# Summing the heads of O during attention for the last eight projection visits, and smaller moves around it, in an adaLN transformer block

## The chip, the cores and the metric

The kernel runs on one core of a Trainium2 chip. The metric is the time of one execution on the device in microseconds; the median of several runs counts. The engines are TensorE (PE in the profile; PEld is its loading of weights), VectorE (DVE), ScalarE (ACT), GpSimd (POOL) and SyncE (SP), whose queue issues almost all DMAs here. Each engine works through its own instructions in the order in which they were issued, and waits on semaphores for the others.

## The reference, cut to what matters

```python
mod = (silu(c) @ w_mod).reshape(1, 6, 1, -1)          # sa, ca, ga, sb, cb, gb
h = layernorm(x) * (1 + ca) + sa                      # x: 2048 x 576
q = (h @ wq), 32 heads of 128; k, v: last 512 keys of 16 cached heads, each used by 2 heads
o = softmax(q k^T * 128 ** -0.5) v                    # per head
x = x + ga * (o @ wo)                                 # wo: 4096 x 576
h = layernorm(x) * (1 + cb) + sb
x = x + gb * ((sigmoid(h @ w_gate) * (h @ w_up)) @ w_down)   # 576 -> 4608 -> 576
```

All in float32.

## The kernel before, in words

A float32 operand of a matmul is split into a high part of a shorter format (F32R) and the rest, and a product is three matmuls: high by low, low by high, high by high (`three`, L280). The split costs an ACT copy (high part) and a subtraction on DVE or POOL (low part).

**Order.** The work is traced in a written order, and a planner then orders the instructions of each engine by when it expects their inputs. An instruction that is pinned (`pin`, L112, and `keep_order`, L108, while `held` is set) stays behind the instruction traced before it on its engine. In attention everything hangs on a step counter n from -8 to beyond N = 512 (loop at L948): `at_n(n, f)` calls f at the beginning of step n, `at_late(n, f)` at its end.

**Attention** (L948 to L978). The 2048 rows are four blocks of 512, in two halves (blocks 0 and 1, then 2 and 3). A unit b is one head on one block (128 in all, `seq` at L415: head by head, in each half), and takes four steps, one for each 128 rows. In step n PE works on q for two units ahead (`qproj`), scores and row maximum for two steps ahead (`scores`; the maximum on DVE, tile neg), the exponential (`expo`, ACT, tile pp), the transposes of this step (`transp`; ACT and DVE split them into ptt) and P times V of the unit before (`pv`, into ot). After a unit's last exponential DVE takes the reciprocal of the sums (rs). It has to be spread over the partitions: `put_rs` and `get_rs` write it to DRAM and read it back as a broadcast tile rb; for the last two units, `spread_rs` (L544) multiplies it into an identity (dg) and `spread_mm` (L549) multiplies that by ones on PE, and ACT copies the result to rb. At the end of `pv` DVE multiplies ot by rb into ov, which holds one head for both blocks, and `put_o` (L556) stores it in oscr.

**Beside attention**, the weights of wo, w_gate, w_up and w_down are combined into the sums that the later products need and split (jobs of `bg_load`, `bg_sums`, `bg_split`, `bg_store`, planned at L817 to L839; they use the four tiles of x, one a room, whose content isn't needed then). `norm_block` (L648) makes the statistics (`ln_stats`, L178), the chain of small DVE operations that turns a variance into 1 / sqrt (`ln_chain`, L192, by bit tricks and three Newton steps), the normalised rows (`ln_apply`) and their transposes for blocks 2 and 3 in the steps before half time. `shift_cols` (L855) makes columns of the second shift.

**Projection of O** (L1263 to L1280). The product by wo goes by a scheme of seven products for a 2 x 2 by 2 x 2 product (rows: two blocks; columns: two halves of 288; inner: even and odd heads). There are 32 visits v: 8 passes over (quarter of the heads q, pair of blocks p) by 4 row tiles t. A visit loads 1 MB of O (`v_load`, L907), makes three sums and one in-place difference of its four planes (`v_sum`, L912), splits seven planes (`v_split`, L925: tile vh, three buffers) and runs seven stages of twelve matmuls, each followed by a DVE add from PSUM to x. `beside(v, s)` (L1220) traces what goes beside stage s: a sum and a split for the next visit and, towards the end, the weights of the next quarter (`w_load`, L893, from wosc, pinned on SP), the statistics of blocks 0 and 1 on DVE and their normalising for the MLP (`early_norm`, `early_scale`, `early_sum`).

**MLP** (L1291 on). For each pair of blocks 36 column blocks of 128, with the same scheme of seven products; weights come 192 KB at a time (`load_w`: sr), are split (`split_w`: sw) and used in `product`. The second pair's rows are normalised meanwhile (`late_load`, `late_tile`, L1187 to L1216) and their parts stored.

Of the kernel before, what the change touches and what calls it, by code (L numbers as in the profile page):

```python
# [44 lines left out]
def adaln_block_kernel(ctx: ExitStack, tc: tile.TileContext, x, k_cache, v_cache, wq, wo, w_gate, w_up, w_down,  # L45
# [127 lines left out]
    def load_x(b):  # L173
        keep_order(nc.sync.dma_start(xs[b], xf[b]))
# [17 lines left out]
    def ln_chain(b, both):  # L192
        sl = slice(0, 2) if both else slice(b % 2, b % 2 + 1)
        mv, y, v, a = [z[:, sl] for z in LN[b][2]]
        yi, vi = y.bitcast(I32), v.bitcast(I32)
        ops = [lambda: nc.vector.tensor_scalar(v, mv[:, :, :, 1], EPS, None, op0=OP.add),
# [6 lines left out]
        ops += [lambda: nc.vector.scalar_tensor_tensor(a, mv[:, :, :, 0], -1.0, y, op0=OP.mult, op1=OP.mult)]  # L203
# [281 lines left out]
    def expo(n):  # L485
# [58 lines left out]
    def spread_rs(b):  # L544
        DG[b] = at.tile([P, TPB, P], F32, tag="qt", name="dg", bufs=2)
        for i in range(TPB):
            nc.vector.tensor_scalar(DG[b][:, i], ident, RS[b][:, i : i + 1], None, op0=OP.mult)

    def spread_mm(b):  # L549
        p = ps_qp()  # L550
        for i in range(TPB):
            nc.tensor.matmul(p[:, i * P : (i + 1) * P], ones, DG[b][:, i], start=True, stop=True)
# [3 lines left out]
    def put_o(b):  # L556
        half, hd, blk = blk_of(b)
        to = oscr[half][hd // 8][:, :, hd // 2 % 4, 2 * (hd % 2) : 2 * (hd % 2) + 2]
        keep_order((nc.scalar if b == NBLK - 1 else nc.sync).dma_start(to, OT.pop((half, hd))))
# [83 lines left out]
    for b in range(2, NB):  # L643
        at_n(N // 2 - 43 + b, load_x, b)
    for b in range(NB):
        at_n(N - 48 + 4 * b, load_x, b)

    def norm_block(b, n_stats, n_apply, n_t, step, sc_, sh_, mul, add):  # L648
# [4 lines left out]
        for k in range(12):  # L653
            at_n(n_stats + TPB + k, ln_some, b, False, k, k + 1)
# [3 lines left out]
    norm_block(2, n1 - 35, n1 - 19, n1 - 14, 2, scale, shift, nc.gpsimd, nc.gpsimd)  # L658
# [10 lines left out]
    EX = {}  # L669
# [10 lines left out]
    def early_scale(t, b):  # L680
        h = xs[b][:, t, :]
        (nc.vector if b else nc.gpsimd).tensor_mul(h, h, rows2["scale"])

    def early_sum(t, k):
        if k == 0 and t % 2 == 0:
            for c in (T1, T2, T4):
                EX[c, t // 2] = hp.tile([P, 2, D2], F32, tag="ts", name="ex", bufs=6)
# [131 lines left out]
    while jobs or wide:  # L819
# [10 lines left out]
        for r in rooms:  # L830
            free[r] = n + {"ab": 10, "tail": 13}.get(kind, 12)
        at_n(n, bg_load, k, rooms)
        for part in range(2):
            at_n(n + 4 + part, bg_sums, k, part)
            if kind != "ab":
                at_n(n + 6 + part, bg_split, k, part)
        for part in range(4 if kind == "tail" else 1):
            at_n(n + (7 if kind == "ab" else 8) + part, bg_store, k, part)
        due = max(due, n - 2) + {"ab": 4.6, "tail": 7.6}.get(kind, 5.9)  # L839

# [13 lines left out]

# [587 lines left out]
```

## Time and profile before

| | |
|---|---|
| median of 3 runs | 3082.87 us (3081.51 to 3083.08) |
| the profiled execution | 3081.02 us, its span 3079.0 us |
| granted TensorE clock, mean | 0.997 |
| instructions | 49150 |
| POOL, ACT busy in the span | 1641.9 us, 1680.2 us |
| DMA packets moved | 558.72 MB, mean 181 GB/s |

A row of the timeline gives start and duration in us, engine, operation, output<-input by the program's tile names, shape, how many were merged, and in brackets how long the engine was idle before it and what ended that. Rows of groups (one line of code, engine, operation, tiles) give the busy us, the mean ns of one, the idle us before them. Every instruction has the line L36, that of the helper that records it, so that tiles tell them apart. SPq is SP issuing a DMA; the duration is the issuing, not the transfer. The granted clock is the share of full speed that TensorE got.

### The profile page before, as it was taken

The numbers are of one execution on the slowest core, as the hardware profiler recorded it, in microseconds if no ns is written. First come the engines' busy times: TensorE is split into PE (matmuls) and PEld (weight loads), VectorE is DVE, ScalarE is ACT, GpSimd is POOL, SyncE is SP. The second block draws the span as 40 slices with busy tenths as digits, with TensorE's granted clock in tenths as the row PEclk, the third lists the DMA queues.
The fourth block names the chain that finished last, engine by engine and source line by source line (L and its number), as shares of the span: only waits on it lengthen the run. The fifth ranks groups of instructions, "written<-read, shape, count | busy, mean of one in ns | idle before, by whom it ended". The sixth has DMA issues, their size and how long they took to land.

```text
span 3079.0 us, 49150 instructions
## 1 busy us (share of the span) xinstructions
PE 3022.5 (98%) x16651; PEld 2600.9 (84%) x16651; DVE 2190.9 (71%) x3872; ACT 1680.2 (55%) x3358; POOL 1641.9 (53%) x1534
## 2 busy tenths in 40 slices
PE   8999999999999999999999999999999999999998
PEld 6888788878888888887999888888888888888887
DVE  6666666677666666667888987666666876666667
ACT  5666666656667676554334454444544545444542
POOL 2334368644577773212555327666655666555654
PEclk9999999999999999999999999999999999999999
DMA  4687778766777777654546535555555564554453
GB/s 124 182 199 213 193 235 249 218 183 185 194 250 249 249 238 185 174 172 169 204 160 263 214 125 173 170 158 163 166 148 142 159 187 135 148 146 142 135 159 100
DMA packets 468795, 558.72 MB, mean 181 GB/s; under 512 B 51136, under 2 KB 421056, under 8 KB 459584
## 3 DMA queue, kind: packets, MB, share of 16 engines
q1 hardware_dynamic: 467408, 555.06, 60.1%
q8 instruction: 132, 2.16, 0.3%
q14 instruction: 119, 0.97, 0.1%
q10 hardware_dynamic: 1136, 0.53, 0.1%
HBM read 388.04 MB, written 167.41 MB: 180 GB/s over the span
## 4 chain that ended last, share of the span: by engine, by line
PE 87%; DVE 5%; POOL 3%; issue 2%; ACT 1%; DMA 1%; SPq 0%; POOLq 0%; ACTq 0%; DVEq 0%
PE a L36 19%; PE st L36 17%; PE qp L36 13%; PE w L36 12%; PE ot L36 11%; PE c L36 10%; PE b L36 5%; DVE x L36 1%; POOL x L36 1%; DVE vh L36 1%; POOL hl L36 0%; PE wo L36 0%; POOL vs L36 0%; DVE neg L36 0%; ACT pp L36 0%
## 5 line engine op out<-in xcount | busy, mean ns | idle before, releaser
L36 DVE TENSOR_TENSOR x<-w,x 128x288 f32<-128x288 f32 x980 | 435.6, 454 | 299.7 <-PE w L36 295.8
L36 PE MATMUL a<-hc,sw 128*128 128x512 f32 x2016 | 584.9, 395 | 9.2 <-POOL sw L36 5.2
L36 DVE TENSOR_REDUCE neg<-st 128x1 f32<-128x512 f32 x512 | 352.7, 689 | 281.1 <-PE st L36 281.1
L36 ACT ACTIVATE ptt<-st 128x512 fp32r<-128x512 f32 x512 | 306.2, 598 | 394.3 <-PE st L36 393.9
L36 PE MATMUL ot<-ptt,vs 128*128 128x512 f32 x1536 | 487.2, 425 | 2.9 <-DVE ptt L36 2.9
L36 PE MATMUL qp<-hTm,wa 128*128 128x512 f32 x1536 | 446.1, 399 | 4.9 <-DVE qt L36 2.8
L36 PE MATMUL st<-kt,qt 128*128 128x512 f32 x1536 | 443.0, 395 | 1.4 <-ACT pp L36 1.4
L36 DVE TENSOR_TENSOR ptt<-st,ptt 128x512 fp32r<-128x512 f32 x512 | 352.2, 688 | 123.4 <-ACT ptt L36 123.0
L36 ACT ACTIVATE sw<-sr 128x384 fp32r<-128x384 f32 x504 | 261.7, 521 | 261.9 <-issue 91.3
L36 PEld LDWEIGHTS a<-hc,sw 128*128 128x128 f32 x2016 | 355.9, 188 | 51.0 <-POOL sw L36 6.5
L36 ACT ACTIVATE pp<-st,neg 128x512 f32<-128x512 f32 x512 | 350.8, 685 | 55.6 <-DVE neg L36 55.1
L36 POOL TENSOR_TENSOR sw<-sr,sw 128x256 fp32r<-128x256 f32 x252 | 195.0, 775 | 325.1 <-ACT sw L36 228.9
L36 PEld LDWEIGHTS qp<-hTm,wa 128*128 128x128 f32 x1536 | 284.2, 188 | 74.2 <-DVE qt L36 8.3
L36 PEld LDWEIGHTS w<-wh,hl 128*128 128x128 f32 x1776 | 299.3, 189 | 54.8 <-DVE x L36 6.0
L36 PEld LDWEIGHTS st<-kt,qt 128*128 128x128 f32 x1536 | 288.5, 189 | 66.6 <-ACT pp L36 2.4
L36 PE MATMUL w<-wh,hl 128*128 128x288 f32 x1776 | 332.9, 298 | 3.4 <-DVE x L36 3.3
L36 POOL TENSOR_TENSOR x<-x 128x256 f32<-128x256 f32 (+3 forms) x334 | 246.9, 758 | 152.0 <-DMA x<-in_B_w_up_dram 88.4
L36 PEld LDWEIGHTS st<-ident,pp 128*128 128x128 f32 x2048 | 255.8, 140 | 78.0 <-issue 7.2
L36 PE MATMUL st<-ident,pp 128*128 128x128 f32 x2048 | 307.9, 273 | 9.2 <-DVE rs L36 6.4
L36 PE MATMUL c<-hc,sw 128*128 128x512 f32 x1008 | 303.8, 394 | 0.0
L36 PEld LDWEIGHTS ot<-ptt,vs 128*128 128x128 f32 x1536 | 253.5, 191 | 29.7 <-DVE ptt L36 4.2
L36 POOL TENSOR_TENSOR hl<-vs,hl 128x512 fp32r<-128x512 f32 x139 | 186.7, 1343 | 98.9 <-ACT hl L36 98.9
(211 smaller groups left out, 5107.1 us busy)
## 6 DMA issues: line engine op xcount, KB each, us to landing
sr<-wsc SPq DMA_DIRECT2D x504, 192.0 KB
wh<-dsc SPq DMA_DIRECT2D x144, 288.0 KB
dsc<-x SPq DMA_DIRECT2D x34, 1008.0 KB
vr<-oscr SPq DMA_DIRECT2D x32, 1024.0 KB
rb<-rscr SPq DMA_DIRECT2D x126, 256.0 KB
wsc<-x SPq DMA_DIRECT2D x36, 896.0 KB
oscr<-ov SPq DMA_DIRECT2D x63, 512.0 KB
wosc<-x SPq DMA_DIRECT2D x32, 1008.0 KB
```

What stands on the lines that cost most here:

```text
L36: i = got(*args, **kw)
```

## The change

- *Sums of O.* For the second half's heads 16 to 31 (quarters 2 and 3, the last eight visits) the three sums and the difference are made on POOL in attention, when a pair of heads is done (`sum_o`, `sum_last`), and stored in sscr; the even head is stored together with the odd one, after the difference was written into it. These visits load the sums (`v_load_sum`) in place of making them; visits before them keep making theirs, all on POOL now.
- *First pair's statistics.* `early_stats` makes them by three ACT operations a tile (sum, mean, sum of squares) in place of bn_stats on DVE; `early_chain` is the same chain on them.
- *Stage 0* of every visit is copied by ACT from its PSUM bank into the bank of stage 5, which adds onto it; the DVE add of stage 0 goes. `early_scale` is on DVE for both blocks.
- *Stores of the second pair's parts* move from `late_tile` to `late_put`, two rounds later, and are pinned; part 6 gets its own tile. Buffers: ts 6 to 4, sw 5 to 6; one more `split_w` at u = 1.
- *End of attention:* `spread_rs` is one multiplication, `spread_mm` one matmul, one or two steps later.
- *Blocks 2 and 3:* x is loaded a row tile at a time, their statistics start a step later for block 2, the chain is pinned.
- *Others:* second part of a split and the store of a job one step later, rooms free a step later; the copies of `shift_cols` come five steps ahead of its transposes; three weight loads of the last quarter four visits earlier.

The diff, cut to its core:

```diff
-    def load_x(b):
-        keep_order(nc.sync.dma_start(xs[b], xf[b]))
+    def load_x(b, t=None):
+        t = slice(0, TPB) if t is None else t
+        keep_order(nc.sync.dma_start(xs[b][:, t], xf[b][:, t]))
...
-                at_late(n - 1, spread_mm, b)
+                at_late(n + (0 if b == NBLK - 2 else 1), spread_mm, b)
             if last_of[half * H + hd] == b:
-                at_late(n + (4 if b == NBLK - 1 else 6), put_o, b)
+                m = n + (4 if b == NBLK - 1 else 6)
+                if not summed(half, hd):
+                    at_late(m, put_o, half, hd)
+                elif hd % 2:
+                    m = n + (4 if b == NBLK - 1 else 5)
+                    at_late(m, sum_o, hd)
+                    m += 1 if b == NBLK - 1 else 2
+                    at_late(m, put_o, half, hd - 1)
+                    at_late(m, put_o, half, hd)
+                    at_late(m, put_sx, hd, (0, 1))
+                    at_late(m + 2, sum_last, hd)
+                    at_late(m + 3, put_sx, hd, (2,))
...
     def spread_rs(b):
         DG[b] = at.tile([P, TPB, P], F32, tag="qt", name="dg", bufs=2)
-        for i in range(TPB):
-            nc.vector.tensor_scalar(DG[b][:, i], ident, RS[b][:, i : i + 1], None, op0=OP.mult)
+        nc.vector.tensor_mul(DG[b], ident[:, None, :].to_broadcast([P, TPB, P]),
+                             RS[b][:, :, None].to_broadcast([P, TPB, P]))
...
-            nc.tensor.matmul(p[:, i * P : (i + 1) * P], ones, DG[b][:, i], start=True, stop=True)
+        nc.tensor.matmul(p, ones, DG[b].rearrange("p i q -> p (i q)"), start=True, stop=True)
...
+    def sum_o(hd):
+        e, o = OT[1, hd - 1], OT[1, hd]
+        sx = at.tile([P, 2, TPB, P], F32, tag="sx", name="sx", bufs=1)
+        SX[hd] = sx[:, 0], sx[:, 1], e[:, :, 0], o[:, :, 0]
+        pin(nc.gpsimd.tensor_add(sx[:, 0], e[:, :, 1], o[:, :, 1]))
+        pin(nc.gpsimd.tensor_sub(sx[:, 1], sx[:, 0], e[:, :, 0]))
+        pin(nc.gpsimd.tensor_sub(e[:, :, 1], e[:, :, 0], e[:, :, 1]))
+    def sum_last(hd):
+        s1, s2, a11, a12 = SX[hd]
+        pin(nc.gpsimd.tensor_sub(a11, a12, s2))
+    def put_sx(hd, ks):
+        for k in ks:
+            keep_order(nc.sync.dma_start(sscr[hd // 8][:, :, k, hd // 2 % 4], SX[hd][k]))
...
     for b in range(2, NB):
-        at_n(N // 2 - 43 + b, load_x, b)
+        for t in range(TPB):
+            at_n(N // 2 - 59 + 8 * b + t, load_x, b, t)
...
-            at_n(n_stats + TPB + k, ln_some, b, False, k, k + 1)
+            at_n(n_stats + TPB + k, ln_some, b, False, k, k + 1, True)
-    norm_block(2, n1 - 35, n1 - 19, n1 - 14, 2, scale, shift, nc.gpsimd, nc.gpsimd)
+    norm_block(2, n1 - 34, n1 - 18, n1 - 14, 2, scale, shift, nc.gpsimd, nc.gpsimd)
...
+    def early_stats(b, t):
...
+        pin(nc.scalar.activation(junk, x, AF.Copy, accum_out=sums))
+        pin(nc.scalar.activation(means, sums, AF.Copy, scale=-1.0 / D))
+        pin(nc.scalar.activation(junk, x, AF.Square, bias=means, accum_out=squares))
...
-        (nc.vector if b else nc.gpsimd).tensor_mul(h, h, rows2["scale"])
+        nc.vector.tensor_mul(h, h, rows2["scale"])
...
-                at_n(n + 6 + part, bg_split, k, part)
+                at_n(n + 6 + 2 * part, bg_split, k, part)
...
+    FROM = VISITS - 2 * TPB
+    def v_load_sum(v, i):
+        q, p, t = VISIT[v]
+        k = (0, 2, 3)[i]
+        VSUM[v, k] = late["b"].tile([P, 4, P], F32, tag="vt", name="vt", bufs=3)
+        pin(nc.sync.dma_start(VSUM[v, k], sscr[q][:, t, i]))
...
     def beside(v, s):
-        if v + 1 < VISITS and s < 4:
+        if v + 1 < FROM and s < 4:
             v_sum(v + 1, s)
...
+        if FROM <= v + 1 < VISITS and s < 3:
+            v_load_sum(v + 1, s)
...
-            elif v == LAST[k] - 2 and s in (1, 3, 5):
+            elif v == LAST[k] - (6 if k == 3 else 2) and s in (1, 3, 5):
                 w_load(k + 1, s // 2)
         if DONE0 - 4 < v <= DONE0 and s in (0, 2):
-            ln_stats(s // 2, v - DONE0 + 3)
+            early_stats(s // 2, v - DONE0 + 3)
...
-            dst = xs[2 * pair + row][:, t, col * D2 : (col + 1) * D2]
-            nc.vector.tensor_add(dst, p, dst)
+            if s == 0:
+                pin(nc.scalar.activation(banks["b"], p, AF.Copy))
+            else:
+                dst = xs[2 * pair + row][:, t, col * D2 : (col + 1) * D2]
+                nc.vector.tensor_add(dst, p, dst)
...
+    def late_put(t):
+        h0, h1, tt, t4 = LATE.pop(t)
         d = scr[1].rearrange("c p t d -> p c t d")[:, :, t, :]
+        for c, v in ((0, h0), (2, tt), (4, h1[:, 1:2]), (5, h1[:, 0:1]), (6, t4[:, 0:1])):
+            pin(nc.sync.dma_start(d[:, c : c + v.shape[1], :], v))
...
+        if u in (6, 11, 16, 21):
+            late_put((u - 6) // 5)
+        if u == 1:
+            split_w()
+            load_w()
```

More of the change, by code (lines that the diff above doesn't have):

```diff
@@ L190, in ln_stats, with chain @@
         nc.vector.bn_aggr(mv[:, t, :], st)
-    def ln_chain(b, both):
-        sl = slice(0, 2) if both else slice(b % 2, b % 2 + 1)
-        mv, y, v, a = [z[:, sl] for z in LN[b][2]]
+    def chain(first, v, y, a, last):
         yi, vi = y.bitcast(I32), v.bitcast(I32)
-        ops = [lambda: nc.vector.tensor_scalar(v, mv[:, :, :, 1], EPS, None, op0=OP.add),
+        ops = [first,
                lambda: nc.vector.tensor_scalar(yi, vi, 1, None, op0=OP.logical_shift_right),
@@ L866, in shift_cols @@
         pin(nc.vector.tensor_sub(fcol[:, 2], fcol[:, 1], fcol[:, 0]))
-    at_n(110, shift_cols)
+    for half in range(2):
+        at_n(100 + half, shift_ends, half)
+    at_n(106, shift_cols)
     lctx = ExitStack()
@@ L946, in adaln_block_kernel @@
         at_n(N - 34 + 2 * s, w_load, 0, s)
-    for n in range(NLO, N + TPB + 2):
+    for n in range(NLO, N + TPB + 4):
         if n == N - 7:
```

101 lines of the change are left out of this document (60 added, 41 removed).

## The prediction

> **What bounds the kernel now.** I read the page first (busy time of the engines), then the waits of PE (TensorE), then the windows around each wait, then the timeline there.
>
> ```profile
> span 3079.0 us, 49150 instructions
> ## 1 busy us (share of the span) xinstructions
> PE 3022.5 (98%) x16651; PEld 2600.9 (84%) x16651; DVE 2190.9 (71%) x3872; ACT 1680.2 (55%) x3358; POOL 1641.9 (53%) x1534
> ```
>
> PE is busy in 3022.5 of 3079.0 us. No matmul is taken out by the change (its sums of O are made on the vector engines, and four small matmuls become one over the same columns), so all that it can win is PE's 56.5 us of idle time and what the clock loses after a long idle. So the limit is 56.5 us, 1.8%, less the waits at the program's start, which aren't touched, and the question is which waits go and which come.
>
> ```profile
> PE st L36 <- DVE rs L36: 6.4, 1, 6.4
> PE c L36 <- DVE x L36: 6.3, 5, 1.9
> PE a L36 <- POOL sw L36: 5.2, 3, 1.7
> ...
> PE qp L36 <- DVE dg L36: 2.9, 5, 0.7
> ...
> PE wo L36 <- POOL hd L36: 1.0, 1, 1.0
> ```
>
> Each row: who waited, on whom, total us, times, longest. They lie in five places, and the change has an edit for each. What the places cost, by windows (start:end, length, then busy us of PE, PEld, DVE, ACT, POOL, then granted clock, DMA share, GB/s):
>
> ```profile
> 665.00:670.00 5.00, 3.79 (x11) 3.23 (x12) 3.01 (x6) 2.15 (x6) 3.20 (x5) 0.50 0.37 64
> 670.00:675.00 5.00, 5.00 (x24) 4.05 (x23) 2.73 (x4) 2.94 (x7) 1.11 (x1) 0.84 0.23 43
> ```
>
> ```profile
> 1440.00:1445.00 5.00, 5.00 (x25) 4.43 (x24) 1.15 (x2) 0.43 (x1) 0.00 (x0) 0.69 0.75 253
> ```
>
> ```profile
> 1500.00:1700.00 200.00, 200.00 (x1510) 200.00 (x1509) 176.11 (x269) 79.69 (x126) 111.77 (x72) 1.00 0.59 223
> ...
> 1715.00:1800.00 85.00, 74.38 (x531) 70.95 (x530) 76.97 (x139) 35.55 (x57) 27.25 (x21) 1.00 0.49 181
> ```
>
> Both stretches are in the projection of O. In 1500 to 1700 PE never waits, though DVE (VectorE) is 88% busy; in 1715 to 1800, the last eight visits, DVE is 91% busy and PE loses 85.00 - 74.38 = 10.6 us. 1510 matmuls in 200 us make 0.1325 us for one and 1.59 us for a stage of twelve; a visit has seven stages, 11.1 us.
>
> **The change part by part.**
>
> *1. Statistics of blocks 2 and 3 in attention (chain pinned, x loaded in quarters).* From the timeline in the 6.4 us wait:
>
> ```profile
> 659.45 1.36 DVE L36 SCALAR_TENSOR_TENSOR ln_a<-ln_a,ln_v 128x4 f32<-128x4 f32 x1
> ```
>
> An operation of the chain, on four columns only, takes 1.36 us here: it isn't its size, it stands beside operations of POOL (GpSimd) in the timeline. Several of these were issued in one bunch, ahead of the row maximum that PE's scores need. Pinned (an instruction is then kept behind its predecessor on the engine), the 24 chain operations go out one a step, and a third of DVE is idle in attention (47.85 of 70 us in the row of part 6). The wait goes, 6.4 us, and with it the clock: (1 - 0.50) x 3.79 + (1 - 0.84) x 5.00 = 2.7 us. Of 9.1 us I take **8.6**; bounds 0 (the bunch forms elsewhere) and 9.1. The eight quarter loads of x in place of two whole ones are six issues more on SP, under half a us each, in a queue with room.
>
> *2. shift_ends ahead of shift_cols.* The 1.0 us wait on the copy "hd" goes, as the copies are made five steps earlier: **1.0**; bounds 0 and 1.0.
>
> *3. The end of attention.* spread_rs becomes one multiply, and the matmul that spreads it comes one to two steps later.
>
> ```profile
> 1421.34 3.22 DVE L36 TENSOR_SCALAR dg<-ident,rs 128x128 f32<-128x128 f32 x4
> ```
>
> ```profile
> 1436.40 0.60 ACT L36 ACTIVATE rb<-qp 128x512 f32<-128x512 f32 x1 [3.98 <-PE qp L36]
> 1436.90 0.59 ACT L36 ACTIVATE ptt<-st 128x512 fp32r<-128x512 f32 x1
> 1437.03 5.96 SPq L36 DMA_DIRECT2D wd<-wosc  x2
> 1437.52 0.69 DVE L36 TENSOR_TENSOR ptt<-st,ptt 128x512 fp32r<-128x512 f32 x1 [1.15 <-ACT ptt L36]
> ...
> 1438.27 4.37 PE L36 MATMUL ot<-ptt,vs 128*128 128x512 f32 x12 [1.90 <-DVE ptt L36]
> ...
> 1442.67 0.69 DVE L36 TENSOR_TENSOR ov<-ot,rb 128x512 f32<-128x512 f32 x1 [4.46 <-PE ot L36]
> ```
>
> Four DVE operations took 3.22 us, PE waited for them (2.9 over both blocks), and ACT (ScalarE) stood 3.98 us in front of the copy rb with the last ptt behind it, which PE then awaited for 1.90. With the matmul behind the last transposes neither happens. What stays is the latency of the last ptt, 0.60 + 0.69 less PE's work beside it, about 1 us. Gain 2.9 + 1.9 - 1.0 = 3.8, and the clock of 0.69 in 1440 to 1445 gives 0.31 x 5 = 1.5: **5.3**; bounds 2 and 6.3.
>
> The same place gets a **new wait**. One POOL sum of this size, and a stretch in which the DMA engines are full:
>
> ```profile
> L36 POOL TENSOR_TENSOR vt<-vr 128x512 f32<-128x512 f32 x6 | 8.3, 1382 | 36.4 <-issue 19.5 <-DVE vh L36 8.8 <-DVE ln_a L36 8.1
> ```
>
> ```profile
> 1750.00:1770.00 20.00, 18.42 (x135) 17.69 (x133) 19.12 (x35) 6.96 (x11) 6.01 (x4) 1.00 0.97 367
> ```
>
> The sums of the last pair can be made only when the last ov is there (1443.4). They are three POOL operations, then the store of the even head, then a fourth POOL operation that overwrites what that store reads, then its store on SP. The loads of weight tiles 5 and 6 (wd) are pinned behind that store; now they are issued at 1437.0 and by 1443.0. Working it out, with 1.38 us a sum and 253 GB/s for 512 KB: sums end at 1443.4 + 4.1 = 1447.5, the store lands at 1450.1, the fourth sum ends at 1451.5, wd starts at 1451.9 and its first 1152 KB land between 1455.2 (at 367 GB/s) and 1456.6 (at 253). The projection starts where PE's last ot ends, 1442.6, so stage 5 wants it at 1442.6 + 5 x 1.59 = 1450.6. PE waits 4.6 to 6.0 us, and stage 6 another 1.6 to 3.1 for the second tile; 6.2 to 9.1 in all.
>
> If two stages of the next visit go ahead of it, 3.2 us less. A wait of that length is like the 6.4 us one, which cost 2.7 us of clock. Bounds 3.3 and 12; I take 7 and 2.7, **9.7 lost**, since PE took nothing ahead in the waits of 6.4 and 1.90 us either. *TensorE: Matmul & The Clock Gate* of the Trainium skill, Part 1, says that the clock halves after an idle window of about 3.4 us; the 0.50 behind a 6.40 us wait agrees, and so does 1.00 in 1715 to 1800, where no wait on DVE is over 1.9 us. By it a wait split in two by hoisted stages would keep the clock, and 2.7 us of the loss would go.
>
> *4. The last eight visits.* What DVE and POOL do there:
>
> ```profile
> L36 DVE TENSOR_TENSOR vh<-vr,vh 128x512 fp32r<-128x512 f32 x27 | 20.6, 764 | 1.9 <-ACT vh L36 1.7
> L36 DVE TENSOR_TENSOR vh<-vt,vh 128x512 fp32r<-128x512 f32 x18 | 17.9, 997 | 0.5 <-ACT vh L36 0.5
> L36 DVE TENSOR_TENSOR x<-a,x 128x288 f32<-128x288 f32 x25 | 11.2, 449 | 0.4 <-PE a L36 0.4
> L36 DVE TENSOR_TENSOR x<-c,x 128x288 f32<-128x288 f32 x14 | 6.3, 448 | 1.0 <-PE c L36 0.9
> L36 DVE TENSOR_TENSOR vt<-vr,vt 128x512 f32<-128x512 f32 x7 | 5.1, 735 | 0.2
> L36 DVE TENSOR_TENSOR vr<-vr 128x512 f32<-128x512 f32 x6 | 5.1, 857 | 3.5 <-POOL vt L36 3.5
> ```
>
> The sums leave DVE (5.1 + 5.1 = 10.2 us) and POOL; stage 0's add becomes an ACT copy (8 x 0.45 = 3.6 off DVE); four multiplications by scale come to DVE (3.0). The 45 vh take 38.5 us; at the 0.69 us of the ptt row they would take 31, and the difference is the waiting beside POOL. Three of the seven loads of the last weights go four visits ahead, out of this stretch. So DVE falls from 77.0 to about 77 - 10.2 - 3.6 + 3.0 - 7.5 = 59 us in 74 us of PE work, 79%, less than the 88% at which PE lost nothing. The wait of 10.6 goes, and late come two new things. ACT gets the statistics of eight tiles in the four visits before: two passes over 576 columns of some 0.8 us each, their accumulator reads and a small one, about 2.2 us (two ptt rows of 0.59 for 512 columns bound it from below, 1.3 us). Beside it stand an ACT copy and a vh of 0.6 each in a stage of 1.59; the vh behind it is then just in time, and I take 1 us lost (0 to 4). And each visit loads 768 KB more, in the visits in which the queue already moves 367 GB/s at 0.97 share: 1.5 us lost (0 to 4). Gain **8.1**; bounds 2.6 and 10.6.
>
> *5. The second pair's stores (late_put) and one more split weight tile.*
>
> ```profile
> 1891.69 1.08 SPq L36 DMA_DIRECT2D scr<-h  x2
> 1892.87 0.89 SPq L36 DMA_DIRECT2D sr<-wsc  x2
> ```
>
> The weight loads sr stood on SP behind stores that waited for POOL's sums; the split weights sw came late, and PE waited 1.7 us. That makes two of the three waits on sw, the third is where the pairs change. Stores two rounds later wait for nothing, and one tile more of sw, a product's time, covers the rest: **4.3** of 5.2; bounds 1.7 and 5.2.
>
> *6. Sums in attention's last quarter.* Four POOL operations of 1.38 us for two heads, that is in 16 of the 512 steps of some 2.8 us that end at 1442, and 768 KB more to store. The even head's store waits for its partner's, which the three buffers of ov allow, and the background jobs on the weights end twelve steps later, by the code's own times still before x is loaded into their rooms. The store on SP waits for three of them (4.1 us), and behind it stand put_rs and get_rs. I cost it at nothing: it is covered by the distance from get_rs to its user.
>
> ```profile
> 1230.80 0.34 SPq L36 DMA_DIRECT2D rb<-rscr  x1
> ```
>
> ```profile
> 1239.97 1.04 DVE L36 TENSOR_TENSOR ov<-ot,rb 128x512 f32<-128x512 f32 x1
> ```
>
> ```profile
> 1060.00:1130.00 70.00, 70.00 (x362) 57.53 (x361) 47.85 (x74) 50.27 (x103) 54.48 (x44) 1.00 0.75 247
> ```
>
> Here rb was issued 9.2 us before ov, one of the tightest cases, and PE has no wait near it. Bounds 0 and 8 x 4.1 = 33 lost.
>
> **The sum.** 8.6 + 1.0 + 5.3 + 8.1 + 4.3 = 27.3 gained, 9.7 lost: 17.6. The profiled execution took 3081.0 (span 3079.0 and 2.0 around it), so 3063.4; the median shown, 3082.87, is 1.9 higher: **3065 us**.
>
> **The rivals.**
> - *PE fills the new wait* or the load isn't late: 3.3 lost or less instead of 9.7, about 3057. Against it: the waits of 6.4 and 1.90 us that PE sat out.
> - *ACT or DMA takes DVE's place* in the last visits, or the bunch of part 1 forms again, so that one edit doesn't do what it says: 8 us are missing, 3073; both, 3081. For it: the schedule is made by a planner that doesn't see POOL's hold on DVE.
> - *A table load for Square.* The one in the trace:
>
> ```profile
> 1826.96 1.28 ACT L36 ACT_TABLE_LOAD   x1
> ```
>
> Square among Copy would need two a tile, 16 x 1.28 = 20.5 us on ACT in four visits of 11.1 us, where it has 44.5 - 4 x 4.8 - 8 x 2.2 = 7.7 to spare (4.8: 40% of a visit in 1500 to 1700 and the copy): 13 us lost, 3078. *ScalarE: Activation LUTs* of the Trainium skill (Table sets) says that a function outside the active set needs a load and names copy and identity, not square, among those in every set. The trace has no Square.
> - *The slower side: SP held in the last quarter.* POOL is 78% busy in 1060 to 1130. If it comes to the sums late, SP stands still until they are done and rb is late for ov. It decides from the point where the delay passes the 9.2 us less the load's own time, about 6 us; then each of the eight pairs shows its 4.1 us to PE: 33 lost, 3065 + 33 = 3098. Against it: the 4.1 us alone, with POOL free, stay below that point, and no PE wait stands in that quarter now.
>
> **Chances.** Forecast (3059 to 3072) 0.50; new wait filled (3050 to 3058) 0.19; an edit that misses (3072 to 3081) 0.17, half of it within 0.2%; table load 0.04, within; slower 0.10, of which 0.02 only just within. Below 3076.7 is faster by over 0.2% (6.2 us), about what this measurement can tell from no change: 0.78; within it 0.14; slower 0.08. The range 3050 to 3082 leaves out the slower case and a little at the low end.
>
> **What would show it.** Right: no wait over 2 us in the stage at 650 to 680 and a clock of 1.00 there; no wait on dg; DVE below 85% and PE full in the last eight visits; waits on sw of at most one; a PE wait of 4 to 9 us about 8 us into the projection, on a DMA of wd. Wrong: PE waits at ot or qp between 1130 and 1430 (SP held), ACT table loads in the visits, or an idle PE where the first pair's products start.

## The result, and the profile after

The changed kernel took 3066.35 us (median of 4 runs, 3064.78 to 3067.26), the kernel before beside it 3082.97 us (3081.51 to 3083.86): a ratio of 0.9946 with a 95% interval of 0.9929 to 0.9963, that is 11 to 22 us less. The page of the changed kernel begins:

```profile
span 3065.5 us, 49332 instructions
## 1 busy us (share of the span) xinstructions
PE 3022.1 (99%) x16639; PEld 2597.5 (85%) x16639; DVE 2147.9 (70%) x3800; ACT 1694.5 (55%) x3430; POOL 1655.5 (54%) x1544
```

PE is busy for the same 3022 us to 0.4 us, and the span is 13.5 us shorter: by this column only idle time went. Matmuls at a lower clock count in it as busy, so it can't show what the clock cost. The rows of PE's waits that are new or changed (who waited, on whom, total us, times, longest):

```profile
PE ot L36 <- DVE ptt L36: 5.3, 7, 3.2
...
PE a L36 <- DVE vh L36: 2.4, 2, 1.7
PE b L36 <- DMA wd<-wosc: 2.3, 1, 2.3
...
PE c L36 <- ACT vh L36: 1.5, 2, 0.8
```

The waits on rs, sw, dg and POOL's hd are gone from the list, and that of stage c on x too. New are a wait of 3.2 us on ptt and a group on vh and wd; the wait of w on x in the MLP grew from 3.3 to 5.2 us. Where they lie shows in a ledger by place. Each length is the distance between the starts of the same two instructions in both traces: the reciprocal rs of a unit of attention, the first matmul of a visit, and in the MLP every 49th matmul that reads sw, which makes a round.

| place | before | after | gained | predicted |
|---|---|---|---|---|
| start to rs of unit 26 | 330.0 | 333.5 | -3.5 | 0 |
| unit 26 to 50 (shift_ends) | 260.8 | 258.9 | 1.9 | 1.0 |
| unit 50 to 100 (blocks 2 and 3) | 553.1 | 545.3 | 7.8 | 8.6 |
| unit 100 to visit 0 (end of attention, and the sums in its last quarter) | 298.5 | 298.1 | 0.4 | 5.3 |
| visits 0 and 1 (new wait) | 22.6 | 35.4 | -12.8 | -9.7 |
| visits 2 to 23 | 245.1 | 244.9 | 0.2 | 0 |
| visits 24 to 31 | 106.8 | 94.0 | 12.8 | 8.1 |
| rounds 0 to 19 of the MLP | 338.4 | 334.5 | 3.9 | 4.3, with the row below |
| round 20 to the end of the span | 923.7 | 920.9 | 2.8 | |

The gains and losses sum to 13.5 us, the difference of the spans. The first row isn't the change's (the last experiment below); without it the sum is 17.0, between the 16.6 of the medians and the 17.6 forecast. The second profile of the kernel before (experiment 12) shows how far such rows vary by themselves: up to 0.9 us in a row behind the first. So the total came out, in part by luck: as gains, the terms of the last eight visits and of the MLP were 4.7 and 2.4 us too small, those of the end of attention and of the new wait 4.9 and 3.1 us too large, and the errors cancelled.

At 665 to 675, where the long wait had been, PE waits 0.27 us in ten and the clock is whole:

```profile
665.00:670.00 5.00, 5.00 (x27) 4.08 (x27) 5.00 (x13) 2.38 (x5) 1.53 (x2) 1.00 1.05 333
670.00:675.00 5.00, 4.73 (x25) 3.73 (x24) 3.82 (x12) 2.69 (x7) 1.49 (x3) 1.00 0.87 233
```

The last eight visits, by windows (columns as in the prediction), over the stretch that the prediction used:

```profile
1715.00:1800.00 85.00, 83.69 (x628) 83.01 (x628) 67.04 (x137) 47.06 (x85) 3.75 (x6) 1.00 0.60 221
```

The busy column rose by 83.69 - 74.38 = 9.3 us, but the number in brackets rose from 531 matmuls to 628: 97 more at 0.1325 us are 12.9 us of work, and the ledger has 12.8. The gain is read from the count.

The seam of attention and projection, in the changed kernel's timeline (start, length, engine, output<-input, in brackets the idle time before and what ended it):

```profile
1413.61 0.53 SPq L36 DMA_DIRECT2D sscr<-ov  x1
1414.24 0.57 SPq L36 DMA_DIRECT2D vr<-oscr  x1
...
1420.71 0.63 ACT L36 ACTIVATE vh<-vr 128x512 fp32r<-128x512 f32 x1 [2.87 <-DMA vr<-oscr]
...
1422.12 0.63 ACT L36 ACTIVATE vh<-vt 128x512 fp32r<-128x512 f32 x1 [0.78 <-POOL vt L36]
1422.66 0.58 ACT L36 ACTIVATE ptt<-st 128x512 fp32r<-128x512 f32 x1
...
1424.29 1.65 PE L36 MATMUL ot<-ptt,vs 128*128 128x512 f32 x3 [3.22 <-DVE ptt L36]
```

The planner put the first copies vh of visit 0 on ACT ahead of a ptt. The load vr that they read was issued at 1414.24, right behind a store of sums (sscr), and its data came 6.5 us later; ACT stood for it, and ptt and PE behind ACT. Twelve us later:

```profile
1436.85 1.28 POOL L36 TENSOR_TENSOR sx<-ov 128x512 f32<-128x512 f32 x1 [10.15 <-DVE ov L36]
...
1439.45 1.75 POOL L36 TENSOR_TENSOR ov<-ov 128x512 f32<-128x512 f32 x1
...
1441.16 1.73 POOL L36 TENSOR_TENSOR vt<-vr 128x512 f32<-128x512 f32 x1
1441.23 0.51 SPq L36 DMA_DIRECT2D oscr<-ov  x1
...
1446.33 1.61 POOL L36 TENSOR_TENSOR vt<-vr,vt 128x512 f32<-128x512 f32 x1
...
1447.90 1.27 POOL L36 TENSOR_TENSOR ov<-ov,sx 128x512 f32<-128x512 f32 x1
1449.20 0.51 SPq L36 DMA_DIRECT2D sscr<-ov  x1
1449.82 1.06 SPq L36 DMA_DIRECT2D wd<-wosc  x2
...
1456.20 2.08 PE L36 MATMUL b<-wd,vh 128*128 128x288 f32 x12 [2.32 <-DMA wd<-wosc]
```

The third sum ends at 1441.2, and the store of the even head (oscr), which the fourth sum has to wait for, is issued then. POOL makes all four sums of visit 1 (1441.16 to 1447.9) before the last pair's fourth; its store and, behind that, wd follow. The trace has the last signal of the even head's store at 1444.4, and the DMA engines move nothing in 1445 to 1450 below. So of the 6.7 us between the third and the fourth sum 3.2 are the wait for that store, and 3.5 the place in POOL's queue. The windows there:

```profile
1440.00:1445.00 5.00, 4.28 (x31) 3.96 (x29) 5.00 (x7) 1.89 (x3) 4.92 (x4) 1.00 0.61 188
1445.00:1450.00 5.00, 2.71 (x12) 2.17 (x11) 1.80 (x3) 0.54 (x1) 4.09 (x3) 0.75 0.00 0
1450.00:1455.00 5.00, 3.62 (x12) 2.95 (x12) 1.52 (x3) 0.72 (x2) 0.00 (x0) 0.57 0.93 320
1455.00:1460.00 5.00, 3.02 (x15) 2.67 (x16) 1.47 (x3) 0.93 (x2) 0.00 (x0) 0.77 1.00 423
1460.00:1465.00 5.00, 5.00 (x24) 5.00 (x24) 0.44 (x1) 0.44 (x1) 3.35 (x3) 0.55 0.49 205
```

94 matmuls in 25 us, where 188 have room at 0.1325 us: 12.5 us lost. PE's idle time is 6.4 of it. The granted clock was 0.55 to 0.77 in four windows; (1 - clock) times the busy time there, as in the prediction, gives 5.2 more.

### The profile page after: what moved, and what is told of

It is laid out like the page before. It is cut to its first block, busy times and chain, and to the rows that moved or that the text cites. A ratio compares the mean times of both kernels' runs of the same rounds, so it can differ in the third digit from the quotient of the medians.

```text
span 3065.5 us, 49332 instructions
## 1 busy us (share of the span) xinstructions
PE 3022.1 (99%) x16639; PEld 2597.5 (85%) x16639; DVE 2147.9 (70%) x3800; ACT 1694.5 (55%) x3430; POOL 1655.5 (54%) x1544
## 4 chain that ended last, share of the span: by engine, by line
PE 90%; DVE 4%; POOL 2%; issue 1%; DMA 1%; ACT 1%; SPq 0%; POOLq 0%; ACTq 0%; DVEq 0%
PE a L36 20%; PE st L36 18%; PE qp L36 13%; PE w L36 12%; PE ot L36 11%; PE c L36 10%; PE b L36 5%; DVE x L36 1%; POOL x L36 1%; DVE neg L36 0%; PE wo L36 0%; DVE v L36 0%; DVE ptt L36 0%; DMA sr<-wsc 0%; POOL hl L36 0%
## 5 line engine op out<-in xcount | busy, mean ns | idle before, releaser
L36 PEld LDWEIGHTS w<-wh,hl 128*128 128x128 f32 x1776 | 298.1, 188 | 59.3 <-DVE x L36 9.2
L36 POOL TENSOR_TENSOR sw<-sr,sw 128x256 fp32r<-128x256 f32 x252 | 188.1, 747 | 296.5 <-ACT sw L36 281.1
L36 PEld LDWEIGHTS ot<-ptt,vs 128*128 128x128 f32 x1536 | 254.1, 191 | 34.9 <-DVE ptt L36 8.0
```

Of the source, the lines that this page charges most:

```text
L36: i = got(*args, **kw)
```

## The experiments

Ratios are against the kernel before on the same chip.

**1. The fourth sum in a tile of its own** (`own_tile`; `s3` has the shape of `e[:, :, 0]`).

```diff
-        SX[hd] = sx[:, 0], sx[:, 1], e[:, :, 0], o[:, :, 0]
+        s3 = at.tile([P, TPB, P], F32, tag="qt", name="s3", bufs=2) if hd == H - 1 else e[:, :, 0]
+        SX[hd] = sx[:, 0], sx[:, 1], s3, o[:, :, 0]
...
-                    at_late(m + 2, sum_last, hd)
-                    at_late(m + 3, put_sx, hd, (2,))
+                    at_late(m - 1 if b == NBLK - 1 else m + 2, sum_last, hd)
+                    at_late(m if b == NBLK - 1 else m + 3, put_sx, hd, (2,))
```

> Edit: for the last pair of heads alone the fourth sum is written to a tile of its own instead of over the even head's, so it no longer waits for that head's store and stands behind the third sum on POOL; its store follows at once, and the loads of weight tiles 5 and 6 (wd) behind it on SP. In the changed kernel the third sum ended at 1441.2, the fourth at 1449.2, wd were issued at 1449.8 and the first landed at 1456.2; the first two visits of the projection took 35.4 us from visit 0's start to visit 2's, against 22.6 before. Theory 1 (the order of POOL and the store ahead of wd make the new wait): fourth sum ends at 1442.7, wd issued by 1443.5, first landing by 1450; PE's waits of 6.3 us in 1444 to 1460 fall to 1 to 3 us, the clock there comes back for most of its 5 us, the two visits take 24 to 28 us, and the time is 3055 to 3059. Theory 2 (rival: the DMA engines are full there, so wd lands when it lands, whoever issues it earlier): issued at 1443.5, landing still after 1455, two visits at 33 us or more, time 3064 to 3067. Theory 3 (rival: POOL's sums for visit 1, which now come 1.5 us later, become the wait): wait on POOL vt or on vh instead, two visits 30 to 35 us, time 3061 to 3066.

Measured: 3057.68 us, ratio 0.9917 (0.9903 to 0.9930). Visits 0 and 1 took 27.1 us. Timeline:

```profile
1438.64 1.74 POOL L36 TENSOR_TENSOR s<-ov,sx 128x512 f32<-128x512 f32 x1
...
1440.40 0.51 SPq L36 DMA_DIRECT2D sscr<-s  x1
...
1441.02 1.07 SPq L36 DMA_DIRECT2D wd<-wosc  x2
...
1447.04 2.32 PE L36 MATMUL b<-wd,vh 128*128 128x288 f32 x12
```

The fourth sum follows the third at once. Visit 0 started 2.5 us earlier in this profile; counted from its start, wd is issued 6.3 us earlier (7.7 us behind it instead of 14.0) and stage 5 starts 6.6 us earlier (13.8 instead of 20.4), though the DMA engines were at a share of 0.99 from 1440 on. Theory 1 holds, and 2 and 3 fall: 8.3 of the 12.8 us came from the fourth sum's delay. The edit takes away both of its parts, the wait for the even head's store and the place behind visit 1's sums, so it doesn't tell them apart; the trace above does.

**2. Visit 0's first copies kept in order on ACT** (`pin_split`).

```diff
-        nc.scalar.activation(t[:, 0], src, AF.Copy)
+        i = nc.scalar.activation(t[:, 0], src, AF.Copy)
+        if v == 0 and s < 3:
+            pin(i)
```

> Edit: the first three copies vh of visit 0 on ACT are kept behind their predecessors on the engine, as the copies ptt of the last steps of attention are. In the changed kernel a copy vh that waited for the load vr stood ahead of a ptt on ACT, and PE waited 3.22 us for that ptt at 1424.3, with a granted clock of 0.86 and 0.50 in the ten us behind. Theory 1 (that order is the wait): the wait goes, with its clock, 3.2 + 3.2 us; the projection starts at about 1429.5 instead of 1435.8; but the loads wd are issued no earlier than the sums of the last pair allow, which move with the projection's start, so the 12.8 us lost behind stay: time 3059 to 3062. Theory 2 (rival: the gain is given back, because wd's landing is bound by the DMA engines and not by the start of the projection): start 6 us earlier, waits of the first visits 6 us longer, time 3065 to 3067.

Measured: 3061.78 us, 0.9927 (0.9914 to 0.9939). The wait on ptt is gone and the projection starts at 1429.7, 6.1 us earlier; visits 0 and 1 still take 34.9 us. Theory 1 holds. That the load vr was late is the other half of this wait; experiment 7 takes that away.

**3. Both edits** (`both`).

> Edit: the last pair's fourth sum in a tile of its own and visit 0's first copies vh kept in order on ACT, together. Alone they gave 3057.7 (own tile) and 3061.8 (order), 8.7 and 4.6 under the changed kernel's 3066.35. Theory 1 (two separate waits at the seam of attention and projection): the projection starts at about 1429.5, four POOL sums end near 1436.5, wd issued at 1437, and of the start's 6 us most is kept, since the DMA engines are no longer full when wd is issued: 3051 to 3054. Theory 2 (rival: both wait for the same loads, so the second edit gives nothing on top of the first): 3057 to 3059, with the first two visits 5 us longer than the own tile's 27.1.

Measured: 3053.53 us, 0.9900 (0.9885 to 0.9915), below the changed kernel's interval. Start of visit 0 at 1430.6, two visits in 26.8 us. Theory 1: the two waits are separate, and their gains of 8.7 and 4.6 us give 12.8 together. It is the best kernel of this study, with the next one beside it.

**4. The last pair's sums on DVE** (`both_dve`): `nc.vector` for `nc.gpsimd` in `sum_o` and `sum_last` where hd is H - 1.

> Edit: as the run before it in this list (tile of its own and order of vh), and the last pair's four sums on DVE instead of POOL. A sum took 1.29 to 1.74 us on POOL and DVE's vh beside them 1.4 us instead of 0.69 in the own-tile run. Theory 1 (the four sums' length is what is left of the wait, and POOL's hold makes vh late): four sums of 0.7 end 3 us after the last ov, wd issued 3 us earlier than with POOL, vh 0.7 us again; first two visits 23 to 25 us, time 3048 to 3051. Theory 2 (rival: DVE's 2.8 us of sums push vh of stages 3 to 6 late): wait on vh instead of wd, time as with POOL, 3051 to 3055.

Measured: 3053.41 us, 0.9900 (0.9886 to 0.9913). wd was issued at 1435.6 instead of 1438.3, and nothing came of it: two visits in 27.0 us. vh took 1.4 us as before, since POOL's sums for visit 1 moved to the same time. A wait of 1.2 us on wd went and one of 0.8 us on vh came. Theory 1 falls; theory 2 has the time, but what made vh long is POOL's sums, not DVE's.

**5. PE's stages in order in visits 0 and 1** (`pe_order`, on top of 4): their matmuls pinned.

> Edit: on the kernel with tile of its own, order of vh and the last pair's sums on DVE (3053.4), the matmuls of visits 0 and 1 are kept in the order of their stages on PE. There wd was issued at 1435.6, 3 to 5 us before it was with POOL's sums, yet visits 0 and 1 took 27.0 us against 22.4 without the last pair's sums: PE's queue holds visit 1's stage 0 ahead of visit 0's stage 5 and stood for its vh (1.67 and 0.72 us). Theory 1 (PE's order is what is left): stage 5 waits 1 to 2.5 us for wd, and stages follow without the waits on vh: visits 0 and 1 take 24 to 26 us, 3050.5 to 3053. Theory 2 (rival: wd lands at 1443 to 1444, full DMA engines, and the order only hid it): stage 5 waits 4 us or more on wd, with the clock, visits 27 to 30 us, 3053.5 to 3056.

Measured: 3054.63 us, 0.9907 (0.9892 to 0.9922); two visits in 28.9 us.

```profile
1434.77 2.21 SPq L36 DMA_DIRECT2D wd<-wosc  x2
1437.03 3.23 SPq L36 DMA_DIRECT2D vr<-oscr  x2
1442.23 2.49 PE L36 MATMUL b<-wd,vh 128*128 128x288 f32 x12 [3.42 <-DMA wd<-wosc]
```

Issued at 1434.8, used at 1442.2: 7.4 us for a load behind three stores. The stages of visit 1 that PE took ahead had covered part of that wait. Theory 2, if wd came a little earlier than it said. Of the 4.4 us that are left (26.8 in experiment 3 against 22.4 in experiment 7) the place is thus known, the load wd, but not why it comes late: in experiment 7 it took about as long (1428.9 to 1435.9) and PE didn't wait, because it was issued 1.7 us before visit 0 and not 5 to 8 us after it.

**6. The old spread of the reciprocals on kernel 3** (`dg4_on_both`): four multiplications, four matmuls, `at_late(n - 1, spread_mm, b)`.

> Edit: on the kernel with the fourth sum in its own tile and vh in order (3053.5), the spread of the last two blocks' reciprocals as before the change: four multiplications of 128 columns and the matmul one to two steps earlier. From the reciprocal of block 126 to the first matmul of the projection it was 21.8 us before, 19.8 in the changed kernel and 13.8 there. Theory 1 (the prediction's term: 5.3 us for this edit, now that the wait on ptt at 1424 no longer hides it): 18 to 20 us there, waits of PE on dg of about 2.9 us, time 3057 to 3059. Theory 2 (rival: the 8 us from 21.8 to 13.8 come from the order of vh on ACT, and the spread is worth 1 us or less): 14 to 15.5 us, 3053.5 to 3055.

Measured: 3056.73 us, 0.9914 (0.9900 to 0.9927); the interval overlaps that of 3, so its places decide: 16.1 us from unit 126 to visit 0 against 13.8 (from unit 100 294.5 against 292.1), waits on dg of 1.0 us, and two visits in 30.4 against 26.8. The spread is worth 2.4 us in its own place, between the theories. Of the 3.6 us in the visits the windows give about 2.7: PE's idle time is 0.5 us more, and the granted clock was 0.84 and 0.50 in 1440 to 1450, where experiment 3 had 1.00 (its waits there were three, 3.6 us in all; here four, 4.1 us). Why it fell here and not there isn't shown, so these 3.6 us are not put down to the spread.

**7. Only quarter 2 summed in attention** (`q2_only`): `sscr` for q = 2 alone, `FROM = VISITS - TPB`.

> Edit: only heads 16 to 23 are summed in attention; heads 24 to 31 are summed in the visits, as before the change, so no sum and no sum's store stands behind the last heads. Theory 1 (the sums of the last pair make the loss at the projection's start; the gain of the last eight visits comes from both passes alike): the first two visits take 22.6 to 24 us instead of 35.4, 11 to 12.8 us won; visits 24 to 27 have their sums back and lose about half of the 13 us that the last eight visits had won, 6.5: time 3060 to 3063. Theory 2 (the gain of the last visits came almost only in visits 24 to 27, 10.2 of 13 us by the starts of the visits, and from their sums): 10 lost, 12 won, time 3063 to 3066. Theory 3 (the gain of the last visits came from the statistics on ACT and the stage 0 copies, not from the sums): nothing lost there, time 3053 to 3056. Rival to all: the first two visits stay at 30 us or more, then it wasn't the sums: 3070 or more.

Measured: 3057.53 us, 0.9912 (0.9899 to 0.9926). Visits 0 and 1 took 22.4 us, so the sums of these heads, of which only the last pair's fall into visit 0, made the whole loss there. The time lies in none of the ranges, because the projection also started 5.2 us earlier than in the changed kernel: the stretch from unit 100 to visit 0 took 292.4 us against 298.1. With no sums and stores of these heads in SP's queue the load vr was issued six us earlier than the 1414.24 above, and PE didn't wait for ptt, though the order on ACT was not pinned:

```profile
1408.28 0.37 SPq L36 DMA_DIRECT2D vr<-oscr  x1
```

Visits 25 and 26, by windows cut at their starts:

```profile
1709.00:1722.00 13.00, 11.80 (x85) 11.18 (x84) 12.32 (x25) 7.06 (x12) 5.17 (x4) 1.00 0.22 74
1722.00:1740.00 18.00, 15.03 (x89) 14.27 (x89) 16.11 (x26) 7.92 (x13) 6.49 (x5) 0.81 0.13 51
```

DVE is 95% and 90% busy there, though no sum runs on it any more: visits 24 to 27 took 53.1 us against 44.6, and visits 28 to 31 as long as in the changed kernel. So theory 2 is right about the visits: 8.5 of the 12.8 us are the sums of visits 24 to 27, when the first pair is normalised on DVE.

**8. The statistics back on DVE** (`stats_dve`): `ln_stats` and `ln_some(0, True, ...)` in place of `early_stats` and `early_chain`.

> Edit: the changed kernel with the first pair's statistics back on DVE (bn_stats and bn_aggr, and the chain from them), nothing else undone. Before the change PE did 503 matmuls in 1720 to 1800 where 612 have room, that is 14.2 us lost, and in 1672 to 1717, where the statistics then ran, DVE was busy 44.12 of 45 us and PE lost only some 0.5. In the changed kernel DVE is busy 33.92 of 45 there. Theory 1 (the sums alone made DVE's loss in the last eight visits; the statistics on ACT bought room that nothing needs): time 3066 to 3068, no new wait in visits 21 to 24. Theory 2 (the statistics' backlog on DVE reached into visits 24 to 27): 3 to 6 us longer, 3069.5 to 3073, with waits of PE on x or vh around 1715 to 1750.

Measured: 3067.33 us, 0.9948 (0.9935 to 0.9960). Visits 24 to 31 take 93.7 us against 94.0. Theory 1: the statistics on ACT give nothing here.

**9. Stores early again** (`stores_early`): `late_put` right behind `late_tile`.

> Edit: the changed kernel with the second pair's parts stored right behind the sums that make them, two rounds earlier, as before; the sixth tile of split weights stays. Theory 1 (the stores that wait for POOL on SP make the weights late, as the prediction has it): the waits on sw at 1897 and 2068 come back at 1.7 us each, with one or two shorter ones for the other two tiles: 3069 to 3071. Theory 2 (rival: the sixth tile alone covers a late weight, a product being 0.9 us): 3066 to 3067, no wait on sw.

Measured: 3067.48 us, 0.9948 (0.9936 to 0.9961), no wait on sw; rounds 4 to 20 are 0.6 us longer. Theory 2, against the prediction.

**10. Five tiles of split weights** (`five_tiles`): `bufs=5` for sw, no extra `split_w` in round 1.

> Edit: the changed kernel with five tiles of split weights instead of six and without the extra split and load in round 1; the later stores stay. In the run with the stores early again and six tiles no wait on sw came back and rounds 4 to 6 took 0.6 us longer. Theory 1 (the sixth tile is what covers the late weights, not the later stores): PE waits on sw of 1 to 2 us come back in 1820 to 2200, two or three of them, and the products take 3 to 5 us longer: 3069 to 3072. Theory 2 (either edit alone covers them): no wait on sw, 3066 to 3067.5.

Measured: 3073.31 us, 0.9971 (0.9960 to 0.9982). Its waits of PE from 1812 to 2200, and the first in its timeline:

```profile
PE a L36 <- POOL sw L36: 4.8, 2, 2.4
```

```profile
1885.15 1.30 POOL L36 TENSOR_TENSOR vs<-g,vs 128x512 f32<-128x512 f32 x1
...
1886.41 1.48 POOL L36 TENSOR_TENSOR hl<-g,hl 128x512 fp32r<-128x512 f32 x1
...
1887.85 1.26 POOL L36 TENSOR_TENSOR hl<-vs,hl 128x512 fp32r<-128x512 f32 x1
1889.08 1.86 POOL L36 TENSOR_TENSOR sw<-sr,sw 128x256 fp32r<-128x256 f32 x2
...
1890.30 0.73 PE L36 MATMUL a<-hc,sw 128*128 128x512 f32 x2 [2.40 <-POOL sw L36]
```

No store stands on SP ahead of these weights, and the waits are back, longer than the 1.7 us of before: POOL comes to the low part of sw only after the sums of the second pair and three operations on the gate's values. Theory 1. Rounds 0 to 19 took 3.7 us more than in the kernel before, which has five tiles and early stores; which of the other edits makes that isn't shown. The edit takes away the extra split and load together with the tile.

**11. Part 1 alone on the kernel before** (`part1_alone`).

> Edit: the kernel before the change with part 1 alone: the statistics' chain of blocks 2 and 3 kept in order, x loaded in quarters, block 2's steps one later. Theory 1 (each part acts in its own place, and the 8.6 us of part 1 reach the end): the 6.4 us wait at 666 goes and the clock stays at 1.00 there; time 3073.5 to 3076 against 3082.9. Theory 2 (rival: the time won at half way is given back where the attention ends, where the weights wd and the last heads wait for other things than PE): the wait goes but the time is 3079 to 3083. The startup of the changed kernel was 3.4 us slower at the first reciprocals; if that comes from part 1's other order of instructions, it shows here, and the time is 3.4 higher.

Measured: 3078.82 us, 0.9985 (0.9977 to 0.9994). From unit 50 to 100 it took 548.5 us, 4.6 less than before and 3.2 more than the changed kernel. What is lost stands in its timeline:

```profile
633.70 0.82 DVE L36 BATCH_NORM_STATS2 st<-x 128x6 f32<-128x288 f32 x2 [3.24 <-DMA x<-in_A_x_dram]
634.44 0.67 DVE L36 TENSOR_TENSOR ptt<-st,ptt 128x512 fp32r<-128x512 f32 x1
...
635.17 1.43 PE L36 MATMUL ot<-ptt,vs 128*128 128x512 f32 x3 [2.40 <-DVE ptt L36]
```

DVE stood 3.24 us for a quarter of x with ptt behind it. The time lies between the ranges of the two theories. The 4.6 us reach the end, as theory 1 says, with a smaller size: the part needs its loads in time, which the changed kernel has.

**12. The kernel before, profiled again** (`before_again`).

> The kernel before, unchanged, profiled once more. In its first profile the reciprocals of block 4 were done at 90.1 us; in the kernel with part 1 alone, whose instructions up to there are in the same order, at 93.2, in the changed kernel at 93.5, and in the others between 91.6 and 93.4. Theory 1 (the first 90 us vary by some 3 us from execution to execution, with the clock and the first loads): another value here, 91 to 94. Theory 2 (something of the change, such as the tiles' places in memory, makes the start slower): 90.1 plus or minus 0.5 again.

Measured: 3083.84 us, 1.0006 (0.9996 to 1.0016); the reciprocal of unit 4 started at 91.7 instead of 90.1, that of unit 26 at 332.1 instead of 330.0. Over all profiles unit 4 spreads from 90.1 to 93.5, also among kernels with the same instructions in the same order up to there (part 1 alone: 93.2). So the start varies from profile to profile by some 3 us (these were taken on more than one chip); of the 3.5 us in the first row of the ledger 3.4 are there by unit 4. The other rows of this second profile agree with the first within 0.9 us: 260.7, 552.2, 299.4, 22.4, 244.5 and 106.9.

## Why the prediction was right, and where not

*1, blocks 2 and 3: right.* 8.6 forecast, 7.8 in the ledger; the wait on rs is gone, and the clock loss behind it. The missing 0.8 are no more than two profiles of one kernel differ by in this row (553.1 and 552.2); small waits on ptt and hd up to 722 are there. Experiment 11 shows the condition that the step left out, a load of x in time.

*2, shift_ends: right*, 1.9 against 1.0. The wait on hd (1.0) is gone; the other 0.9 lies outside the bound of 1.0 and is not traced.

*3, the end of attention: this step failed in its size and in what it named as late next.* dg no longer holds anyone. But the prediction named ptt's latency of about 1 us as what is late next; it was vh on ACT, in front of ptt, for a load of vr. Its wait and clock cost 6.1 us (experiment 2), and with it gone the place gains 298.5 - 292.1 = 6.4 (experiment 3). That is more than the 5.3 forecast, but the edit of the spread is not worth as much: undone alone on kernel 3, it costs 2.4 us in its place (experiment 6). What makes the other 4.0 isn't shown. The prediction asked who waits behind the sums' stores for rb and for wd, but not for vr, which SP issues behind them too (experiment 7).

*3, the new wait: right in place and cause, too small, and its own steps partly wrong.* The three sums took 4.4 us (4.1 forecast). The fourth I let end when the even head's store had landed, 4.0 us after the third; it ended 8.0 after: the store landed 3.2 us after the third sum, and then four sums of visit 1 went first. wd took 6.4 us from issue to use, not 3.3 to 4.7. The price was in the trace before, where the first wd was issued at 1437.03 and gave its last signal at 1443.9, 6.9 us later; the prediction reckoned from the bytes and the GB/s instead. What makes a load last so long isn't shown. Against that, PE took two stages of visit 1 ahead, which I had ruled out from two waits in which it couldn't. So the sign that I had named, one wait of 4 to 9 us on wd, didn't come: there were five waits of 0.7 to 2.3 us, one of them on wd. 12.8 us were lost, 9.7 forecast, and 12 was the bound.

The clock is where the two accounts differed. *TensorE: Matmul & The Clock Gate* of the Trainium skill, Part 1, was the reason for thinking that a wait split by hoisted stages would keep the clock. Here the longest single wait is 2.32 us, below the page's 3.4, and the clock still fell to 0.55. The kernel before had shown as much in a row of the prediction, 0.69 in 1440 to 1445 behind a wait of 1.90. The same page says that the window in which activity is judged runs freely; that fits two runs with the same pair of waits, 0.72 and 1.67 us, in front of visit 1's stage 0: the own tile got a clock of 0.69 in the window behind it, the sums on DVE 1.00.

```profile
1445.00:1450.00 5.00, 5.00 (x28) 4.71 (x28) 1.15 (x2) 1.17 (x2) 1.70 (x2) 0.69 1.00 419
```

```profile
1445.00:1450.00 5.00, 5.00 (x39) 4.83 (x38) 2.66 (x5) 1.93 (x4) 1.81 (x2) 1.00 0.92 388
```

*4, the last eight visits: right, and mis-sized by my reading.* I took the limit from the busy column, 85.00 - 74.38 = 10.6. By the count it is 85 - 531 x 0.1325 = 14.6, and 12.8 came, above the bound. DVE's load came as reckoned: 67.04 us of 85, 79%, as forecast, and a vh fell to the 0.69 that I had taken from ptt:

```profile
L36 DVE TENSOR_TENSOR vh<-vr,vh 128x512 fp32r<-128x512 f32 x28 | 19.3, 690 | 4.0 <-ACT vh L36 3.7
L36 DVE TENSOR_TENSOR vh<-vt,vh 128x512 fp32r<-128x512 f32 x23 | 15.8, 689 | 4.9 <-ACT vh L36 4.7
L36 DVE TENSOR_TENSOR x<-a,x 128x288 f32<-128x288 f32 x22 | 10.0, 455 | 4.3 <-PE a L36 4.1
```

It was 764 and 997 ns beside POOL's sums. The operation with one input in PSUM, x<-a,x, took 449 ns beside them and 455 without. This agrees with *SBUF — State Buffer* of the Trainium skill, section "Who interferes with whom": a DVE operation with both inputs in SBUF and a POOL operation that reads SBUF exclude each other. So what the sums cost DVE was in good part their running on POOL: in experiment 7 no sum was on DVE, and the visits with sums still took 53.1 us, where the kernel before, with some of them on DVE, took 54.7. What the copy of stage 0 on ACT and the scaling on DVE give was not tried alone. Of the losses that I set against it (1 for ACT, 1.5 for the loads) nothing shows up to visit 28; 1.3 us of idle time are left at 1774 to 1778, on vh. The statistics on ACT are no part of the gain (experiment 8).

*5, the stores: wrong in cause, and near in size by luck.* 3.9 us in rounds 0 to 19 and 6.7 in the whole MLP, against 4.3 with a bound of 5.2. I gave the weight to SP's stores and called the sixth tile the rest. Experiments 9 and 10 turn it round: without the later stores 0.6 us is lost, without the sixth tile 7.4 (rounds 4 to 20). The row of SP that I quoted was true, and beside the point: POOL's queue was as late. In the kernel before ACT waited for the load sr, and POOL came free for the low part at the same time:

```profile
1894.86 1.30 POOL L36 TENSOR_TENSOR hl<-vs,hl 128x512 fp32r<-128x512 f32 x1
...
1895.44 1.00 ACT L36 ACTIVATE sw<-sr 128x384 fp32r<-128x384 f32 x2 [4.65 <-DMA sr<-wsc]
1896.09 1.64 POOL L36 TENSOR_TENSOR sw<-sr,sw 128x256 fp32r<-128x256 f32 x2
```

The 2.8 us gained from round 20 on lie in the last round and the end of the program, 36.2 us before and 32.9 after. The ten profiles with six tiles took 32.4 to 34.0 there, the four with five tiles 34.5 to 36.4; so the gain goes with the tile (and the extra split made with it), and how is not traced.

*6, sums in the last quarter: right.* No wait on rb appears; what there is of a loss, 1.6 us from unit 100 to 126, is in the order of DVE's reciprocals as much as in PE's time, which stays open.

*Rivals.* No table load came with Square, the ACT group is the same in both kernels:

```profile
L36 ACT ACT_TABLE_LOAD x2 | 2.6, 1283 | 1.9 <-issue 1.8
```

SP was not held until rb was late. "PE fills the new wait" was half true: it filled it with two stages, 3.2 us at full clock, and the wait was longer by more.

## What to carry to other kernels

Where work is moved to the seam of two stages, list what each in-order engine has queued there by the planner's order, not by data: the two largest misses here were an ACT copy in front of one that PE needed and a POOL sum, behind a store and four other sums, that a weight load stood behind, and two small edits won 12.8 us. Read what a stage loses from the count of matmuls times the time of one; the busy column gave too little here, 10.6 us for 14.6. Take a load's time from a load of that size in the trace, not from bytes and GB/s. When two edits are aimed at one wait, undo each alone before giving one of them the credit.

## What the hardware showed that I had not expected

- Around five waits of 0.7 to 2.3 us within 15 us the granted clock was 0.55 to 0.77 in four windows; 5.2 of the 12.5 us lost there are clock. Three waits of 0.7, 1.7 and 1.2 us within 6 us left it at 1.00 in experiment 3.
- A DVE subtraction of 128x512 with both inputs in SBUF takes 0.69 us alone and 1.4 to 1.5 beside POOL's sums in experiment 1; one with an input in PSUM doesn't change (0.44 to 0.46).
- Statistics of a 128x576 tile on ACT took 0.67 + 0.77 us for the two passes, 0.19 for each of the two accumulator reads and 0.20 for the mean, 2.0 us in all.
